# A fused SSD scan and gated feed-forward layer: the first scan in another order, and the state part of y reading the states in the scan's own tile

## The chip, the cores and the metric

The kernel runs on one core of a Trainium2 chip. The metric is the device time of one execution, in microseconds (us), over three executions: 352.07 us is their median. A core has five engines that run at the same time, each with its own list of instructions in a fixed order: TensorE (PE in the profile; its weight loads are shown apart as PEld), VectorE (DVE), ScalarE (ACT), GpSimd (POOL) and SyncE (SP), which here issues transfers. They wait for one another by semaphores.

## The reference

Two layers, one after the other, all in fp32. The first is a state-space scan (Mamba-2's SSD) for 4 sequences, 8 heads, 768 tokens, head size D = 32 and state size N = 16. The reference steps over chunks of 32 tokens:

```python
cum = np.cumsum(log_a, axis=-1)
L = np.exp(cum[:, :, :, None] - cum[:, :, None, :]) * causal
M = np.einsum('bhin,bhjn->bhij', Cc, Bc) * L
y_intra = np.einsum('bhij,bhjd->bhid', M, xc)
y_inter = np.einsum('bhin,bhnd->bhid', Cc, state) * np.exp(cum)[..., None]
y[:, :, sl] = y_intra + y_inter
decay_from_j = np.exp(cum[:, :, -1:] - cum)
Bx = np.einsum('bhjn,bhjd->bhjnd', Bc, xc) * decay_from_j[..., None, None]
state = np.exp(la.sum(-1))[:, :, None, None] * state + Bx.sum(axis=2)
```

The heads are then laid side by side, so that y is a matrix of 3072 tokens by 256, and the second layer is applied: `h = y @ w_in` (256 x 2048), `g = h * sigmoid(1.702 h)`, `out = g @ w_out` (2048 x 256).

## The kernel before

**Units of work.** The tokens are cut into six groups of 512 (`TG`). The scan works on pairs of 128-token chunks: pair p is 256 tokens, and a group has two pairs (`PG`). The chunks of the recurrence are 64 tokens (`H`), not 32, so a group has eight states. The 128 partitions hold the eight heads as four strips of 32 partitions (`r`, L-names `rows`), two heads (`q`) to a strip, 16 state elements each. A TensorE operation on one strip uses a tile of 32 rows, and four strips run side by side.

**What a group costs.** A group's y goes through `hidden` (L889: 16 slices of the 2048 hidden columns, SiLU on ScalarE) and a projection. Group 0 and part of the rest do this directly. The later groups use a product scheme with fewer multiplications (L945, L955, L1050, L1057), which needs more additions on VectorE and ScalarE. Nearly all of the time goes there.

**The weights** arrive as pairs of 32-bit words (float64) and are turned into fp32 on the chip, piece by piece: `fetch` has SyncE issue the transfers of a piece, `fields` (L192 and the line after it) cuts out exponent and mantissa on VectorE, `clamp` (ScalarE, two activations) moves the exponent, `rounded` (L208, VectorE) adds the low word, `join` (VectorE) puts it together in `w_in`. Piece 0 holds the first two hidden slices, piece 1 the third and fourth.

**Group 0's scan** is what happens before the first hidden matmul. The decays `a` are loaded, a logarithm and a cumulative sum give `cum`. Then, by engine:
- TensorE builds `cum_i - cum_j` plus a mask in PSUM for the two pairs (`mask_banks` L548, `differ` L554). Ahead of the last of them stand nine tiny matmuls, `pads` (L432), that compute nothing that is used.
- ScalarE takes the exponential (`decay_exp`, L575), which gives `L`.
- VectorE transposes C and B of the group (`turn_first`, L615). `mask_first` makes `CT`, a copy of C for each of the strip's two heads in which the other head's 16 rows are zero; `part` is the column of ones and zeros for it. GpSimd does it for both pairs (L650); for pair 1 VectorE writes one column first (L649).
- TensorE transposes B back (`turn_back`, L627), VectorE multiplies it by the decay to the end of its chunk (`ends_first`, L468, tile `Be`).
- `score` (L682, tile `cb`): C times B for every token pair of a chunk; between the two pairs' matmuls stands `since_first` (L512 on TensorE, L517 the exponential on ScalarE): the decay since the start of each chunk, tile `since`.
- `weigh` (L693, VectorE): `L` times `cb`, one instruction for each pair.
- `gain` (L713, TensorE, two PSUM banks `A`): what each chunk adds to its state, `Be` times x. Both heads of a strip are multiplied with both heads' x, so two of the four quarters of each 32 x 64 block are not wanted.
- `parts_first` (L730, ScalarE): copies `A` into `steps`, a tile [128, 64, 8] in which the eight chunks of one element lie next to each other.
- `drops` (L522, ScalarE): writes into `drop` the decay that belongs to each element of `steps`, with a zero (L724) at the first chunk of each.
- `keep_first`: one VectorE scan (L735) over `steps` and `drop` turns the eight increments into the eight states. Then ScalarE (L743, head 0) and VectorE (L744, head 1) copy the states of each pair into tiles `S`, [128, 4, 64], where the 64 elements of one state lie together, and multiply by `part`, which zeroes the unwanted quarters.
- `since_start` (L667, GpSimd, tile `CsT`): C times `since`.
- `finish`: `intra` (L833), `L` times x, into four PSUM tiles `y0_0` to `y0_3`; two of them reuse the banks that `gain` wrote and `parts_first` reads. Then `inter` (L821): the state as weights (`lhsT`, 32 rows by 64 columns), `CsT` as the moving operand, added to the same tiles. ScalarE copies the result to `yT`, and `hidden` can start. In group 1's `hidden` the 512 columns of the first two `k` steps are cut into four matmuls each, those of the next three into two.

**What sets the order.** Each engine runs its instructions in the order in which the program text issues them; the semaphores between engines follow from the tiles. The order at the end of the function (from L1166) is thus the order on each engine. The transfers for pieces 1 to 5 are issued by SyncE (`fetch(1, held=True)` and the loop after it). A one-element VectorE memset at the head of `fetch(1)` (L171) stands behind `weigh(0)`, and SyncE's transfers of that piece wait for it.

Of the kernel before, what the change touches and what calls it, by code (L numbers as in the profile page):

```python
# [16 lines left out]
P = 128  # L17
# [18 lines left out]
def kernel(  # L36
# [31 lines left out]
    nc = tc.nc  # L68
# [4 lines left out]
    NB, NH, S, D = x.shape  # L73
# [6 lines left out]
    NK = DM // P  # L80
# [4 lines left out]
    PG = CG // 2  # L85
    R = 4
    Q = NH // R
# [10 lines left out]
    ssd = ctx.enter_context(tc.tile_pool(name="ssd", bufs=2))  # L98
# [89 lines left out]
    def fields(i):  # L188
        hi, cols = bits[i][1], slice(0, PIECES[i][2] * DM)
        mantissa[i] = wide.tile([P, PN], U32, tag="m", name=f"m{i}")[:, cols]  # L190
        power[i] = wide.tile([P, PN], U32, tag="p2", name=f"p2{i}")[:, cols]
        nc.vector.tensor_scalar(out=power[i], in0=hi, scalar1=0x7FF00000, scalar2=None,  # L192
                                op0=ALU.bitwise_and)

        nc.vector.tensor_scalar(out=mantissa[i], in0=hi, scalar1=0x000FFFFF,
                                scalar2=0x00100000, op0=ALU.bitwise_and, op1=ALU.bitwise_or)

    def clamp(i):


        e = power[i]
        z = e.bitcast(FP32)
        nc.scalar.activation(z, e, AF.Relu, scale=-8.0, bias=edge[:, 0:1])
        nc.scalar.activation(e, z, AF.Relu, scale=-1.0, bias=edge[:, 1:2])

    def rounded(i):

        nc.vector.scalar_tensor_tensor(out=mantissa[i].bitcast(FP32), in0=bits[i][0],  # L208
                                       scalar=2.0 ** -32, in1=mantissa[i],
                                       op0=ALU.mult, op1=ALU.add)  # L210
# [65 lines left out]
    for r in range(R):  # L276
        (nc.sync, nc.scalar)[r % 2].dma_start(
            out=az0[32 * r:32 * r + 32].rearrange("p k s -> p (k s)"),
# [54 lines left out]
    def fold_ident(k, engine=nc.vector):  # L333
# [12 lines left out]
        out=cum.rearrange("p k s -> p (k s)"), data0=carry.rearrange("p k s -> p (k s)"),  # L346
# [13 lines left out]
    def pick_a(p):  # L360
# [34 lines left out]
    state = {}  # L395
# [69 lines left out]
    def ends_first(p):  # L465

        t = ssd.tile([P, R, 2 * Q, N], FP32, tag="Be", name=f"Be{p}", bufs=3)
        nc.vector.tensor_tensor(  # L468
            out=t, in0=rb[p],
            in1=flat[p].rearrange("p r (e i) -> p r e i", i=H)[:, :, :, H - 1:H].to_broadcast(  # L470
                [P, R, 2 * Q, N]), op=ALU.mult)
        BE[p] = t.rearrange("p r (k q) n -> p k r (q n)", k=2), t
# [46 lines left out]

    def drops():  # L520

        nc.scalar.copy(  # L522
            drop[:, :, 1:], since[0][:, :CG].rearrange("p c (s i) -> p (c s) i", s=2)[:, 1:, H - 1].unsqueeze(
                1).to_broadcast([P, Q * D, 2 * CG - 1]))

# [44 lines left out]
    def decay_exp(p, r, t):  # L570
        if p not in flat:
            L = ssd.tile([P, R, 2 * Q * H], FP32, tag="L", name=f"L{p}", bufs=3)
            flat[p] = L
            Ls[p] = L.rearrange("p r (k q i) -> p k r q i", k=2, q=Q)
        nc.scalar.activation(flat[p] if r is None else flat[p][:, r], t, AF.Exp)  # L575
# [46 lines left out]
    def turn_back():  # L622

        o = bank("b").rearrange("p (j r k e) -> p j r k e", j=PG, r=R, k=2)
        for p in range(PG):
            for k in range(2):
                nc.tensor.transpose(out=o[:, p, :, k], in_=st[p]["BT"][:, k], identity=ident)  # L627
            rb[p] = o[:, p].rearrange("p r k (q n) -> p r (k q) n", q=Q)
# [15 lines left out]
    def mask_first(p):  # L644

        s = st[p]
        s["CT"] = ssd.tile([P, 2, Q, P], FP32, tag="CT", name=f"CT{p}")
        if p:
            nc.vector.memset(s["CT"][:, 0, 0, :1], 0.0)  # L649
        nc.gpsimd.tensor_tensor(  # L650
            out=s["CT"], in0=s["tp"].unsqueeze(2).to_broadcast([P, 2, Q, P]),
            in1=part.unsqueeze(1).unsqueeze(3).to_broadcast([P, 2, Q, P]), op=ALU.mult)
# [8 lines left out]
    def since_start(p, engine=nc.vector):  # L661

        b, c = divmod(2 * p, NC)
        s = st[p]
        tp = s["tp"]
        s["CsT"] = ssd.tile([P, 2, P], FP32, tag="CsT", name=f"CsT{p}", bufs=3)
        engine.tensor_tensor(out=s["CsT"], in0=tp, in1=since[b][:, c:c + 2], op=ALU.mult)  # L667

    def score(pairs, between=lambda: None):

        cb = area(f"cb{pairs[0]}").rearrange("p r (k e) -> p r k e", k=2 * PG)
        for n, p in enumerate(pairs):
            s = st[p]
            BT, CT = s["BT"], s.pop("CT")
            s["cb"] = cb[:, :, 2 * n:2 * n + 2]
            if n:
                between()
            for k in range(2):
                for i, side in enumerate(SIDES):
                    for r in range(R):  # L680
                        rows = slice(32 * r, 32 * r + 32)
                        nc.tensor.matmul(  # L682
                            out=s["cb"][side, r, k].rearrange("p (q i) -> p q i", q=Q),
                            lhsT=BT[rows, k, side], rhs=CT[rows, k, :, side],
                            start=True, stop=True, tile_position=(32 * r, H * i),
                            skip_group_check=True)
# [38 lines left out]

    def parts_first():

        to = steps.rearrange("p e (c s) -> p s c e", s=2)
        for i in range(2):
            nc.scalar.activation(to[:, i], increment[0][i], AF.Copy)  # L730

    def keep_first():

        flat_steps = steps.rearrange("p e m -> p (e m)")
        nc.vector.tensor_tensor_scan(  # L735
            out=flat_steps, data0=drop.rearrange("p e m -> p (e m)"), data1=flat_steps,
            initial=0.0, op0=ALU.mult, op1=ALU.add)
        o = steps.rearrange("p (q d) m -> p q m d", q=Q)
        for p in range(PG):
            state[p] = ssd.tile([P, 4, Q * D], FP32, tag="S", name=f"S{p}", bufs=3)  # L740
            to = state[p].rearrange("p m (q d) -> p q m d", q=Q)
            m = slice(4 * p, 4 * p + 4)
            nc.scalar.activation(to[:, 0], o[:, 0, m], AF.Copy, scale=part[:, 0:1])  # L743
            nc.vector.tensor_scalar(out=to[:, 1], in0=o[:, 1, m], scalar1=part[:, 1:2], scalar2=None,  # L744
                                    op0=ALU.mult)

    def keep_both(pairs, by_scalar=False):

# [129 lines left out]
    def hidden(g, f):  # L878
        j, i = divmod(f, 2)
        if i == 0:  # L880
            block(g, j)
        h = bank(f"h{g}_{f}")
        for k in range(NK):
            n = 2 if g == 1 and NK * f + k < 5 else 1
            if n == 2 and NK * f + k < 2:
                n = 4
            for e in range(n):
                cols = slice(e * TG // n, (e + 1) * TG // n)
                nc.tensor.matmul(out=h[:, cols], lhsT=w_in[:, f, k], rhs=yT[g][:, k, cols],  # L889
                                 start=(k == 0 and e == 0), stop=(k == NK - 1),  # L890
                                 skip_group_check=True)

        nc.scalar.activation(gT[g, j][:, i], h, AF.Silu, scale=GELU_SCALE)
# [263 lines left out]
    def dense(n):  # L1157
        if n:
            t = bank("dense")
        for i in range(n):  # L1160
            nc.tensor.matmul(out=t[:, :4 * H], lhsT=ones,
                             rhs=ones[:, :H].unsqueeze(1).to_broadcast([P, 4, H]),
                             start=True, stop=True, skip_group_check=True)
# [4 lines left out]
        mask_banks(0, r, both[:, r])  # L1168
    for r in range(R):
        if r == R - 1:  # L1170
            pads(9, busy)
        mask_banks(1, r, bank(f"ab1_{r}"))
    turn_first("C")
    turn_first("B")
# [3 lines left out]
    mask_first(0)  # L1178
    for r in range(R):
        decay_exp(1, r, ab[1, r])  # L1180
    fields(0)
    mask_first(1)
    turn_back()
    ends_first(0)
    ends_first(1)
    score(range(PG), since_first)
    weigh(0)
    fetch(1, held=True)
    for i in range(2, 6):
        fetch(i)  # L1190
    rows_a(az, (nc.sync,))
    weigh(1)
    rounded(0)
    drops()
    gain(range(PG))
    parts_first()
    for p in range(PG):
        since_start(p, nc.gpsimd)
    clamp(0)
    keep_first()  # L1200
    dense(2)
    finish(range(PG))
    dense(0)
# [241 lines left out]
```

## Time and profile before

| what | value |
|---|---|
| three executions | 350.84, 352.07, 352.60 us; median 352.07 us |
| the profiled execution, its own time | 349.68 us |
| its span, from the first instruction to the last | 347.8 us |
| PE busy | 342.0 us, 98% of the span |
| weight loads (PEld) busy, beside PE | 271.9 us, 78% |
| DVE busy | 253.5 us, 73% |
| ACT busy | 153.1 us, 44% |
| POOL busy | 12.9 us, 4% |
| granted TensorE clock, mean | 1.000 |

The profile is of one execution. "Busy" is the time in which an engine had an instruction under way; matmuls are pipelined, so a busy TensorE isn't one at its peak. The chain of waits follows the last instruction of the program back: at each step to what released it, or to the instruction before it on its engine; "issue" is time in which an engine waited for nothing that the profile shows, and a name like DVEq is an engine's sequencer. In a line of a group, `out<-in` names the tiles, then come the sizes (partitions x elements), and a bracket gives the idle time before the group and what ended it. L numbers are lines of the kernel before.

### The profile page before, as it was taken

How to read it: one execution, taken by the hardware profiler on the slowest of the kernel's cores; microseconds unless marked ns; L12 is line 12 of the kernel's file. 1: busy time of each engine (PE TensorE's matmuls, PEld its weight loads, DVE VectorE, ACT ScalarE, POOL GpSimd, SP SyncE). 2: the span in 40 equal slices, each digit the busy share in tenths (PEclk: the TensorE clock that was granted, in tenths of full speed). 3: DMA queues.
4: the chain of work that ended last, by engine and by line, in shares of the span. 5: the costliest groups of instructions: out<-in, count | busy, mean ns of one | idle time of the engine just before them, and what ended most of it. 6: DMA issues, size and time to landing. Idle time of an engine off the chain costs nothing.

```text
span 347.8 us, 8141 instructions
## 1 busy us (share of the span) xinstructions
PE 342.0 (98%) x3392; PEld 271.9 (78%) x3392; DVE 253.5 (73%) x479; ACT 153.1 (44%) x349; POOL 12.9 (4%) x41
## 2 busy tenths in 40 slices
PE   8899999999999999999999999999999999999996
PEld 6644444557788888888888888888888888899996
DVE  5899999998679998839995649787555654455463
ACT  5698573107354324744332543442444321554320
POOL 8300000000000100000000000000000000000000
PEclk9999999999999999999999999999999999999999
DMA  6699997435526100435613036300000300000301
GB/s 162 142 336 193 283 212 155 81 77 93 105 58 128 33 2 15 63 104 102 101 28 50 2 81 117 64 2 1 2 2 2 61 2 0 0 2 0 62 0 61
DMA packets 89980, 25.92 MB, mean 75 GB/s; under 512 B 73432, under 2 KB 87128, under 8 KB 89944
## 3 DMA queue, kind: packets, MB, share of 16 engines
q1 hardware_dynamic: 89112, 24.88, 33.3%
q10 hardware_dynamic: 832, 0.52, 0.5%
q8 instruction: 26, 0.43, 0.5%
q14 instruction: 10, 0.08, 0.1%
HBM read 22.15 MB, written 3.24 MB: 73 GB/s over the span
## 4 chain that ended last, share of the span: by engine, by line
PE 97%; ACT 1%; DVE 1%; issue 0%; DVEq 0%
PE acc L1050 28%; PE X L945 20%; PE Y L955 14%; PE h L889 10%; PE o L987 8%; PE acc L1057 7%; PE y L833 2%; PE y L821 2%; PE cb L682 2%; PE A L713 1%; PE busy L440 1%; PE ab L554 1%; PE ab L548 0%; DVE steps L735 0%; ACT steps L730 0%; ACT drop L522 0%
## 5 line engine op out<-in xcount | busy, mean ns | idle before, releaser
L950 ACT ACTIVATE ac<-X 128x256 f32<-128x256 f32 x76 | 29.1, 383 | 78.6 <-PE X L945 78.2
L1050 PE MATMUL acc<-mg,mw 128*128 128x256 f32 x192 | 54.5, 379 | 0.0
L922 ACT ACTIVATE gT<-gT 128x512 f32<-128x512 f32 (+1 forms) x76 | 39.3, 520 | 34.1 <-DVE gT L1077 33.4
L1077 DVE TENSOR_TENSOR gT<-Y,ac 128x512 f32<-128x512 f32 x38 | 26.2, 689 | 36.1 <-PE Y L955 30.5
L945 PE MATMUL X<-my,mi 128*128 128x256 f32 x152 | 45.2, 380 | 0.0
L1077 DVE TENSOR_TENSOR gT<-Y,b 128x256 f32<-128x256 f32 x38 | 15.8, 419 | 35.2 <-PE Y L955 35.2
L1050 PEld LDWEIGHTS acc<-mg,mw 128*128 128x128 f32 x192 | 36.5, 190 | 5.0
L1050 PE MATMUL acc<-gT,w_out 128*128 128x256 f32 x128 | 35.5, 379 | 0.0
L889 PE MATMUL h<-yT,w_in 128*128 128x512 f32 (+2 forms) x98 | 35.5, 518 | 0.0
L945 PEld LDWEIGHTS X<-my,mi 128*128 128x128 f32 x152 | 28.0, 190 | 4.1 <-ACT ac L950 0.4
L889 PEld LDWEIGHTS h<-yT,w_in 128*128 128x128 f32 x98 | 17.0, 190 | 16.5 <-issue 14.3
L987 PE MATMUL o<-gT,w_out 128*128 128x512 f32 x64 | 28.6, 597 | 0.0
L913 DVE TENSOR_TENSOR mg<-gT 128x512 f32<-128x512 f32 x40 | 27.2, 681 | 0.0
L1050 PEld LDWEIGHTS acc<-gT,w_out 128*128 128x128 f32 x128 | 24.2, 190 | 3.4 <-ACT yT L860 0.2
L950 ACT ACTIVATE b<-X 128x256 f32<-128x256 f32 x38 | 14.6, 384 | 20.0 <-PE X L945 19.6
L945 PE MATMUL X<-yT,w_in 128*128 128x256 f32 x76 | 23.2, 389 | 0.0
L945 PE MATMUL X<-my,w_in 128*128 128x256 f32 x76 | 22.7, 382 | 0.2 <-issue 0.2
L955 PE MATMUL Y<-yT,w_in 128*128 128x256 f32 x76 | 22.7, 381 | 0.0
L955 PE MATMUL Y<-my,mi 128*128 128x256 f32 x76 | 22.6, 379 | 0.0
L955 PE MATMUL Y<-yT,mi 128*128 128x256 f32 x76 | 22.5, 379 | 0.0
L987 PEld LDWEIGHTS o<-gT,w_out 128*128 128x128 f32 x64 | 11.8, 190 | 13.2 <-issue 12.7
L402 DVE TENSOR_TENSOR_SCAN L<-a,idents 128x1024 f32<-128x1024 f32 x9 | 20.5, 2277 | 0.4 <-DMA a<-scratch 0.4
(156 smaller groups left out, 544.2 us busy)
## 6 DMA issues: line engine op xcount, KB each, us to landing
a<-scratch SPq DMA_DIRECT2D x18, 256.0 KB, 5.3
bits<-in_moe_w_out_dram SPq DMA_DIRECT2D x8, 512.0 KB, 5.4
x<-in_x_dram SPq DMA_DIRECT2D x24, 128.0 KB, 3.0
out_dram<-ob SPq DMA_DIRECT2D x40, 64.0 KB, 1.9
bits<-in_moe_w_in_dram SPq DMA_DIRECT2D x8, 256.0 KB, 4.6
bits<-in_moe_w_in_dram SPq DMA_DIRECT2D x4, 512.0 KB, 9.3
b<-in_B_dram SPq DMA_DIRECT2D x20, 64.0 KB, 3.0
af<-in_a_dram SPq DMA_DIRECT2D x3, 384.0 KB
```

The lines of the kernel that those rows point to most:

```text
L402: nc.vector.tensor_tensor_scan(out=L, data0=ra[p].rearrange("p k e -> p (k e)"), data1=idents.rearrange("p h i -> p (h i)"), initial=0.0, ...
L682: nc.tensor.matmul(out=s["cb"][side, r, k].rearrange("p (q i) -> p q i", q=Q), lhsT=BT[rows, k, side], rhs=CT[rows, k, :, side], start=Tru ...
L889: nc.tensor.matmul(out=h[:, cols], lhsT=w_in[:, f, k], rhs=yT[g][:, k, cols], start=(k == 0 and e == 0), stop=(k == NK - 1), skip_group_ch ...
L913: nc.vector.tensor_tensor(out=t[:, 0:2], in0=B[:, :, 1], in1=B[:, 0], op=ALU.subtract)
L922: nc.scalar.activation(o, i, AF.Silu, scale=GELU_SCALE)
L945: nc.tensor.matmul(out=s["X"], lhsT=lhsT, rhs=rhs, start=i == "1", stop=i == "4", skip_group_check=True)
L950: nc.scalar.activation(copy, s["X"], AF.Copy)
L955: nc.tensor.matmul(out=o, lhsT=lhsT, rhs=rhs, start=s.pop("new", False), stop=i != "5", skip_group_check=True)
L987: nc.tensor.matmul(out=o[c], lhsT=w_out[:, c, f], rhs=gT[g, f // 2][:, f % 2], start=(f == 0), stop=(f == NF - 1), skip_group_check=True)
L1050: nc.tensor.matmul(out=acc[g][0][i][:, cols], lhsT=w, rhs=h[:, cols], start=(j == 0 and k == 0 and (i, 0) in begins), stop=(j == NF // 2 - ...
L1057: nc.tensor.matmul(out=o[k] if type(o) is list else o[:, cols], lhsT=h[:, cols], rhs=w, start=(j == 0 and (i, k) in begins), stop=(j == NF ...
L1077: nc.vector.tensor_tensor(out=o, in0=v, in1=w, op=ALU.add)
```

## The change

Ten edits, nearly all in group 0's scan:
1. `drops` runs on GpSimd instead of ScalarE.
2. `CT` of pair 1 is made by VectorE in two instructions (one for each head, C times a column of `part`), not by GpSimd; the one-column memset goes.
3. `parts_first` is four ScalarE activations instead of two, one for each half chunk and head, and each multiplies by `part`. So the unwanted quarters are zero before the scan.
4. The copies L743 and L744 behind the scan go. `state[p]` is a view into `steps`: the weights of `inter` are read there, with a step of eight fp32 elements (32 bytes) from one column to the next. Pair 2, in the next group, reads the last of these states in the same way.
5. `since_first`, `drops` and both `since_start` move up to right after `turn_back`, ahead of `ends_first` and `score`; `since_first` no longer stands between the two pairs' `cb` matmuls.
6. `mask_first(1)` stands ahead of `fields(0)`.
7. `clamp(0)` stands ahead of `weigh(0)`, and so, on ScalarE, ahead of `parts_first`.
8. `rounded(0)` stands behind the scan instead of ahead of `gain`.
9. `pads` is 15 tiny matmuls instead of 9.
10. In group 1's `hidden`, the first three `k` steps are cut into two matmuls each, none into four, and the fourth and fifth not at all.

```diff
     def drops():
-        nc.scalar.copy(
+        nc.gpsimd.tensor_copy(
             drop[:, :, 1:], since[0][:, :CG].rearrange("p c (s i) -> p (c s) i", s=2)[:, 1:, H - 1].unsqueeze(
                 1).to_broadcast([P, Q * D, 2 * CG - 1]))
...
         if p:
-            nc.vector.memset(s["CT"][:, 0, 0, :1], 0.0)
+            for q in range(Q):
+                nc.vector.tensor_scalar(out=s["CT"][:, :, q], in0=s["tp"], scalar1=part[:, q:q + 1],
+                                        scalar2=None, op0=ALU.mult)
+            return
         nc.gpsimd.tensor_tensor(
...
     def parts_first():
-        to = steps.rearrange("p e (c s) -> p s c e", s=2)
+        to = steps.rearrange("p (q d) (c s) -> p s q c d", s=2, q=Q)
         for i in range(2):
-            nc.scalar.activation(to[:, i], increment[0][i], AF.Copy)
+            o = increment[0][i].rearrange("p c (q d) -> p q c d", q=Q)
+            for q in range(Q):
+                nc.scalar.activation(to[:, i, q], o[:, q], AF.Copy, scale=part[:, q:q + 1])
...
         for p in range(PG):
-            state[p] = ssd.tile([P, 4, Q * D], FP32, tag="S", name=f"S{p}", bufs=3)
-            to = state[p].rearrange("p m (q d) -> p q m d", q=Q)
-            m = slice(4 * p, 4 * p + 4)
-            nc.scalar.activation(to[:, 0], o[:, 0, m], AF.Copy, scale=part[:, 0:1])
-            nc.vector.tensor_scalar(out=to[:, 1], in0=o[:, 1, m], scalar1=part[:, 1:2], scalar2=None,
-                                    op0=ALU.mult)
+            state[p] = steps.rearrange("p e m -> p m e")[:, 4 * p:4 * p + 4]
...
-            n = 2 if g == 1 and NK * f + k < 5 else 1
-            if n == 2 and NK * f + k < 2:
-                n = 4
+            n = 2 if g == 1 and NK * f + k < 3 else 1
...
-            pads(9, busy)
+            pads(15, busy)
...
+    mask_first(1)
     fields(0)
-    mask_first(1)
     turn_back()
+    since_first()
+    drops()
+    for p in range(PG):
+        since_start(p, nc.gpsimd)
     ends_first(0)
     ends_first(1)
-    score(range(PG), since_first)
+    score(range(PG))
+    clamp(0)
     weigh(0)
...
     weigh(1)
-    rounded(0)
-    drops()
     gain(range(PG))
     parts_first()
-    for p in range(PG):
-        since_start(p, nc.gpsimd)
-    clamp(0)
     keep_first()
+    rounded(0)
```

More of the change, by code (lines that the diff above doesn't have):

```diff
@@ L737, in keep_first @@
             initial=0.0, op0=ALU.mult, op1=ALU.add)
-        o = steps.rearrange("p (q d) m -> p q m d", q=Q)
         for p in range(PG):
-            state[p] = ssd.tile([P, 4, Q * D], FP32, tag="S", name=f"S{p}", bufs=3)
-            to = state[p].rearrange("p m (q d) -> p q m d", q=Q)
-            m = slice(4 * p, 4 * p + 4)
-            nc.scalar.activation(to[:, 0], o[:, 0, m], AF.Copy, scale=part[:, 0:1])
-            nc.vector.tensor_scalar(out=to[:, 1], in0=o[:, 1, m], scalar1=part[:, 1:2], scalar2=None,
-                                    op0=ALU.mult)
+            state[p] = steps.rearrange("p e m -> p m e")[:, 4 * p:4 * p + 4]
     def keep_both(pairs, by_scalar=False):
```

## The prediction

> **What bounds the kernel now.** I read the chain of work that ended last first, by engine, because it says whether the end is set by one engine:
>
> ```profile
> PE 97%; ACT 1%; DVE 1%; issue 0%; DVEq 0%
> ```
>
> The rest is in the first 18 us. From the first hidden-layer matmul (L889, at 17.79) TensorE is busy without a gap worth naming: 42.00 of the 42 us from 18 to 60, 40.00 of 40 from 60 to 100, 244.81 of 248 after that (busy time by stretch). The granted clock is 1.00 in every stretch. So the change is worth what it moves the start of L889, as long as the weights that L889 reads keep up. Second view: the same chain in order of time, from 9 to 18 us.
>
> ```profile
> 10.00 0.68 PE rows L512 x4
> 10.68 0.65 ACT since L517 x2
> ...
> 11.35 1.01 ACT drop L522
> 12.36 1.02 ACT steps L730 x2
> ...
> 13.64 0.69 DVE m L208
> 14.32 1.15 DVE steps L735
> ...
> 15.49 0.59 DVE S L744 x2
> ...
> 16.12 1.68 PE y L821 x54
> 17.79 0.68 PE h L889
> ```
>
> The columns are start and duration. Three things stand there that the change takes out: `drop` on ScalarE, `m` (L208) ahead of the scan (L735), and the state copies (L744, L743 beside it) between scan and state part (L821). Third view: the timeline of the engines around it.
>
> ```profile
> 11.36 2.36 DVE L693 TENSOR_TENSOR L<-L,cb 128x1024 f32<-128x1024 f32 x2 [1.12 <-PE cb L682]
> 12.27 1.11 ACT L730 ACTIVATE steps<-A 128x256 f32<-128x256 f32 x2
> 15.49 0.94 ACT L743 ACTIVATE S<-steps,part 128x128 f32<-128x128 f32 x2 [0.90 <-DVE steps L735]
> 15.49 0.58 DVE L744 TENSOR_SCALAR S<-steps,part 128x128 f32<-128x128 f32 x2
> 17.69 0.43 DVE L192 TENSOR_SCALAR p<-bits 128x512 uint32<-128x512 uint32 x1
> ```
>
> The reader should see that VectorE is nearly as late as ScalarE: `weigh` (L693) ends at 13.72, L730 at 13.38. Taking `drop` away alone gains nothing.
>
> **The change part by part.** Each term against this execution: span 347.8, its own time 349.68.
>
> *Six more pads* (9 to 15). The 18 records of the nine pads take 0.37 with 0.21 for one, so about 9 ns each; 12 more records put the next group (L554) 0.1 later, and with it the exponentials and `turn_back`. The clock is granted in full already, so I count no gain.
>
> *Rows first, C's second mask by VectorE.* Transposes start 0.1 later, at 8.82; the next group follows 0.59 later as now (8.72 to 9.31). `rows` goes there: 9.41 instead of 9.93. `since` follows 0.73 after `rows` (9.93 to 10.66), so 10.14 to 10.80, about 0.5 earlier. The two `cb` groups come after it at about 10.04, without the 0.33 wait for GpSimd's mask and with fewer changes of tile shape (each shows 0.17 to 0.2 of "issue"): the second ends about 11.16 instead of 11.25. `weigh(0)` waits for the last matmul of the second group in both kernels, so it starts 0.09 earlier, at 11.27. VectorE pays two 128x256 masks, 0.295 each by the nearest row (L341), between `turn_first` and `fields`; the covers are its own wait of 1.12 for `cb`, and for the first hidden weights the stretch up to 15. Without that cover it would cost 0.5.
>
> *`drop` to GpSimd.* 448 elements with a strided source are in no GpSimd row. Bounds: 0.56 at the rate of a memset (L540, 256 in 0.32), 1.3 at that of L667 (256 in 0.74). It waits for `since` and ends by 12.2 at the latest, and the two L667 behind it by 13.7; the scan wants `drop` at 13.8 and L821 wants L667's result at 15.5. Cost nothing; the cover is 1.6 us.
>
> *`clamp(0)` ahead of `parts_first`.* 1.43 of ScalarE (13.16 to 14.59), now from about 10.7 to 12.1. It fills the wait for `gain`, which does not move: its last matmuls began at 11.81, just after the last `x` transfer signalled at 11.77. So `parts_first` starts at 12.27, as now.
>
> *`parts_first` in four.* The same 512 elements in the same strided pattern, with a scale. Lower bound 1.11 (the two now), upper 4 x 0.66 = 2.64 if nothing overlaps. Starts lie 0.20 apart for L767 (64 elements, eight in 1.70) and 0.42 for L743 (128 elements, strided on one side). I take 0.34, nearer to L743: 12.27 + 3 x 0.34 + 0.52 = 13.81, which is **0.43 later** than now.
>
> *The scan without L208 before it.* It needs `weigh(1)` (13.55) and `parts_first` (13.84 with the wait): 13.84 instead of 14.24, ends 15.06 instead of 15.46. L208 comes after it, 0.60, and `join(0)` starts at 15.66 instead of 15.99.
>
> *The state copies go.* 0.59 of VectorE and 0.94 of ScalarE. What is late next is not the scan but the intra-chunk part on TensorE (L833): two of its four PSUM tiles take over the banks that `parts_first` reads, one half each, and the last of these is free only when `parts_first` ends. Now its second wave starts at 13.42 and ends at 15.42, with a pause of 0.63 in it (14.05 to 14.69) that the trace puts to "issue". From 13.86 it ends at 15.22 without that pause, 15.85 with it; I take 15.5. So L821 starts at **15.5 instead of 16.12: 0.62 gained**.
>
> *L821 reads the states where the scan left them*, one element in eight, 32 bytes apart. No matmul or weight load in this trace reads like that, so its price is bounded. Now a weight load pays 0.89 ns a column (190 ns for 128 columns at L889, 133 for 64 here), and L821 goes in 28 rounds of 52 ns, which is one load of 64 columns: 1.46 us from first start to last. Below, a strided load is free: 1.46. Above, the rows are the two engines that read this very tile with this step. VectorE: L744 takes 331 ns for 128 elements, a 12-element copy (L357) 170, so 1.39 ns an element. ScalarE: L743's starts are 0.42 apart for 128 elements, as far as L659's are for 256 contiguous ones (four in 1.70), so twice the price an element, about 1.9 ns; with nothing set aside as fixed it is 3.3 ns. I take VectorE's 1.39, as it lies between free and ScalarE's: 64 x 1.39 = 89 ns a round, 2.49 us, **1.03 lost**.
>
> [...]
>
> *Sum.* 15.5 + 2.49 + 0.2 to the next tile shape = 18.19 for L889 instead of 17.78: +0.41. A wait of 0.03 at the third hidden slice (weights ready at 21.19, matmul at 21.34) goes: -0.03. The split in `hidden(1)`: 16 records 0.112 apart become 8 that are 0.2155 apart: -0.07. Pair 2 reads the last state with stride in four matmuls, two rounds: +0.06. Together **+0.37**: 350.05 for this execution. The profiled execution is 2.39 below the median of the three runs, 352.07; the same shift on that gives 352.4.
>
> **The rivals.**
>
> *A. Strided loads are free.* L889 could start at 15.5 + 1.46 + 0.2 = 17.16. But the third slice's weights then bound: VectorE's L192 at 17.69 followed a transfer that signalled at 17.59, and that transfer is issued after `weigh(0)`, which moves only 0.09. So the 0.62 on TensorE shrinks to 0.12, with the split -0.2: 351.9. [...] Against: L743 and L744.
>
> *B. ScalarE's 1.9 ns holds.* 122 ns a round, 3.4 us; L889 at 19.1, +1.3 in all: 353.4.
>
> *C. Slower by more than 0.5%.* The weight loads pay L743's whole 3.3 ns a column: 210 ns a round, 5.9 us; L889 at 21.6: +4.0 with pair 2's rounds, 356.1. This decides once a round passes 135 ns, that is 2.1 ns a column. For it: nothing overlaps a load here, since each round is exactly one load. Against: VectorE reads the same tile at 1.39.
>
> *D. The four `parts_first` do not overlap.* They end at 14.91; L833 at about 16.6, L889 at 19.3: +1.5, 353.6.
>
> *E. The change does not shorten the chain:* scan and intra part wait for `parts_first`, so taking out `drop` and L208 yields nothing. That is within the forecast already (0.40 at the scan, 0.62 at L821).
>
> **How the numbers follow.** Forecast 36%, A 33%, B 12%, C 13%, D 6%. The forecast's own range is 351.7 to 353.0. The range takes in A to D without C and the spread of the runs shown (350.84 to 352.6): 350.8 to 354.5, with C's 13% and a few per cent below left out. 0.5%, 1.76 us, is about what a measurement of this kernel can tell from no change. No case is faster by that much; I leave 7% for something not seen. Slower by it: C, and the top of B and D, 18%. Within it: 75%.
>
> **What would show it.** In the profile after: `since` near 10.1; `parts_first` ending near 13.8; scan at 13.8, right behind `weigh`; L821 starting near 15.5, and its records 89 ns a round (52 if A, 122 if B, over 135 if C); L889 at 18.2. I would be wrong if L833 is late for another reason than `parts_first`, if VectorE's masks delay Be beyond 11.1, or if TensorE gets gaps after 18 us that it does not have now.

## The result and the profile after

The changed kernel takes 352.86 us (median of 22 executions, 351.12 to 355.24); the kernel before, run beside it, 351.26 us (median of 22, 349.70 to 353.27). The ratio is **1.0049, with a 95% interval of 1.0035 to 1.0063**: about 1.7 us slower. The forecast was +0.37 us, with a range (350.8 to 354.5) that holds the measured time. That its 352.4 us lies so near to 352.86 is luck: it was counted from the median of three executions, 352.07, and the median of 22 is 351.26.

The profile after is of the longest of those 22 executions (355.24 us, span 353.4). One thing in it has to be set aside first. TensorE got its full clock at 10.34 us (4.37 in the profile before); this is where the trace's record of a full clock begins, and for the time ahead of it, which has no record, the profile prints 1.00. Ahead of 10.34 the same matmuls are slower: L554 takes 4.22 us instead of 2.59, and everything behind it stands 2.6 us later. L548's matmuls start 0.213 us apart there, and 0.109 apart behind the 4.37 us of the profile before. In the nine other profiles with fifteen pads in which the full clock is recorded it came between 4.15 and 6.57, so the late clock seems to belong to that execution rather than to the change. So I compare from the first matmul of `turn_back` (L627) on, which both kernels reach with all earlier work done. The chain of waits of the changed kernel, start and duration:

```profile
11.29 0.65 PE b L627 x4
11.94 0.65 PE rows L512 x4
12.60 1.14 PE cb L685 x63
13.73 0.79 PE A L716 x53
14.52 1.06 PE dense L1158 x4
15.58 1.02 PE y L832 x63
16.60 0.14 issue
16.73 0.84 PE y L832 x52
17.58 3.08 PE y L820 x56
20.66 6.59 PE h L886 x11
```

ScalarE and VectorE are gone from this chain: neither `drop`, nor `m`, nor the scan, nor copies of the states stand in it. From turn_back to the first hidden matmul it is TensorE alone, and the largest piece is the state part, L820, at 3.08 us (1.68 before). The first hidden matmul comes 9.30 us after turn_back; before it was 9.06. Shares by engine of the whole chain say the same:

```profile
PE 98%; issue 0%; DVE 0%; ACT 0%
```

The second thing to see is the granted clock in the stretches around the state part (columns: stretch, length, busy time of TensorE with its matmuls, clock, DMA share, GB/s):

```profile
17.17:20.58 3.41, 3.41 (x90) 1.00 0.99 258
20.58:23.99 3.41, 3.41 (x6) 0.50 0.95 290
24.00:27.00 3.00, 3.00 (x8) 1.00 1.09 385
```

Right behind the state part the clock is halved for 3.41 us: six hidden matmuls where at full clock there are eight in 3.0. That is not chance in this one execution. The mean clock of an execution tells whether it had such a stretch (3.41 us at half speed in 350 gives 0.995): **16 of the 22 executions of the changed kernel had it, and 15 of the 81 of the kernel before whose clock is listed.** The 16 take 353.38 us on average, the other six 351.94. In the kernel before, the 15 are 0.46 us longer on average than the other 66; no profile shows where in them the clock was low.

### The profile page after: what moved, and what is told of

Read it like the earlier page. It is cut to its first block, busy times and chain, and to the rows that moved or that the text cites. A ratio compares the mean times of both kernels' runs of the same rounds, so it can differ in the third digit from the quotient of the medians.

```text
span 353.4 us, 8142 instructions
## 1 busy us (share of the span) xinstructions
PE 347.3 (98%) x3392; PEld 275.0 (78%) x3392; DVE 253.4 (72%) x478; ACT 151.7 (43%) x348; POOL 12.9 (4%) x41
## 4 chain that ended last, share of the span: by engine, by line
PE 98%; issue 0%; DVE 0%; ACT 0%
PE acc L1047 27%; PE X L942 19%; PE Y L952 14%; PE h L886 10%; PE o L984 8%; PE acc L1054 7%; PE y L832 3%; PE y L820 2%; PE cb L685 2%; PE A L716 1%; PE ab L554 1%; PE busy L440 1%; PE ab L548 1%; PE dense L1158 0%; PE tp L597 0%
## 5 line engine op out<-in xcount | busy, mean ns | idle before, releaser
L1074 DVE TENSOR_TENSOR gT<-Y,b 128x256 f32<-128x256 f32 x38 | 15.8, 418 | 35.9 <-PE Y L952 35.9
L886 PE MATMUL h<-yT,w_in 128*128 128x512 f32 (+1 forms) x86 | 37.0, 587 | 0.0
```

The costliest lines, as they stand in the source:

```text
L1074: nc.vector.tensor_tensor(out=o, in0=v, in1=w, op=ALU.add)
```

## The experiments

Theory (load and clock): a weight load that reads one element in eight is slow (L820 goes in rounds of 120 ns, L821 before in rounds of 52), and the long, thin stretch that this makes leads to the halved clock. Rival one (start): the loss is at the start of the kernel, in the pads and the order. Rival two (order): the halved clock comes from the new order, not from the reads. Each ratio is to the kernel before, run beside the kernels of the same batch (e1 to e4, e5 to e8, e9 to e12), each batch on a chip of its own.

The table gives, from the one profile of each kernel, when the full clock came, when turn_back and the first hidden matmul began, the time between these two, and the state part from its first matmul's start to its last's; then the executions with a mean clock below 0.9975 and the ratio to before.

| kernel | full clock | turn_back | hidden | between | state part | clock lowered | ratio (95%) |
|---|---|---|---|---|---|---|---|
| before | 4.37 | 8.72 | 17.78 | 9.06 | 1.46 | 15 of 81 | 1 |
| changed | 10.34 | 11.29 | 20.59 | 9.30 | 2.88 | 16 of 22 | 1.0049 (1.0035-1.0063) |
| e1 | 4.49 | 9.10 | 17.96 | 8.86 | 1.46 | 0 of 12 | 1.0018 (0.9996-1.0040) |
| e2 | 4.49 | 9.16 | 19.16 | 10.00 | 2.87 | 7 of 12 | 1.0026 (1.0007-1.0045) |
| e3 | 6.04 | 9.55 | 18.20 | 8.65 | 1.63 | 0 of 12 | 0.9995 (0.9976-1.0015) |
| e4 | 6.25 | 9.56 | 18.07 | 8.51 | 1.46 | 0 of 12 | 1.0015 (0.9996-1.0033) |
| e5 | 6.12 | 9.56 | 19.29 | 9.73 | 2.87 | 1 of 1 | one execution |
| e6 | 4.83 | 9.05 | 17.39 | 8.34 | 1.50 | 0 of 1 | one execution |
| e7 | 4.85 | 9.06 | 19.80 | 10.74 | 4.31 | 5 of 7 | 1.0190 (1.0165-1.0214) |
| e8 | not recorded | 9.52 | 18.19 | 8.67 | 1.63 | 0 of 12 | 0.9992 (0.9974-1.0010) |
| e9 | 4.15 | 8.71 | 17.27 | 8.56 | 1.46 | 1 of 12 | 1.0008 (0.9979-1.0037) |
| e10 | 6.01 | 9.42 | 17.73 | 8.31 | 1.46 | 0 of 12 | 0.9956 (0.9933-0.9979) |
| e11 | 6.57 | 9.66 | 24.28 | 14.61 | 7.73 | 6 of 6 | 1.0302 (1.0260-1.0345) |
| e12 | 5.16 | 9.21 | 17.73 | 8.52 | 0.83 | 2 of 12 | 1.0050 (1.0022-1.0078) |

### e1: the copies put back

```diff
-            state[p] = steps.rearrange("p e m -> p m e")[:, 4 * p:4 * p + 4]
+            state[p] = ssd.tile([P, 4, Q * D], FP32, tag="S", name=f"S{p}", bufs=3)
...
+            nc.scalar.activation(to[:, 0], o[:, 0, m], AF.Copy, scale=part[:, 0:1])
+            nc.vector.tensor_scalar(out=to[:, 1], in0=o[:, 1, m], scalar1=part[:, 1:2], scalar2=None,
+                                    op0=ALU.mult)
```

> The changed kernel, with the two copies behind the scan put back, so that the states are read without gaps again; all other edits stay. [...] Then the rounds of L821 are 52 ns again, the first hidden matmul comes about 8.7 us after turn_back (9.4 changed, 9.1 before), the mean clock is 1.000 in nearly all executions, and the ratio to before is 0.997 to 1.001. Rival one (start): the loss is at the start, where TensorE is at half speed until 10.3 us in the profile after, and the later dip is chance: ratio 1.004 as in the changed kernel, whatever L821 does. Rival two (order): the dip comes from the new order, not from the reads: clock 0.995 in most executions still, ratio 1.003 to 1.005.

Measured: 351.79 us (median of 12), ratio 1.0018. The clock is 1.000 or 0.999 in all 12, the state part is back at 1.46 us. So in the changed kernel the halved clock is due to the reads, as the theory has it, and rival two falls. But the ratio is above what the theory gave: with the reads mended, about 0.6 us of loss may be left (the interval reaches from none to 1.4). Its chain shows where a part goes:

```profile
15.18 5.42 DMA bits<-in_moe_w_in_dram
...
20.69 0.43 DVE p L192
21.12 0.34 DVE m L195
21.46 0.61 DVE p L222
...
22.09 0.70 DVE w_in L228
...
22.93 2.38 PE h L892 x5
```

The third hidden slice (L892 at 22.93) could have begun at 21.5 and waits for its weights. L192 here is `fields` of piece 2, which waits for the transfer of piece 2 (20.60), and `join` of piece 1, the one that the third slice needs, stands behind it on VectorE. The execution without the slow reads is held by the next thing in line. This would also explain why the six executions of the changed kernel at full clock (351.94 on average) are no slower than e1 (351.96): the slow loads' time there would lie beside this wait. That is argued, as no profile shows one of the six.

### e2: the reads alone

The kernel before, with `parts_first` in four as in the change, and:

```diff
-            nc.scalar.activation(to[:, 0], o[:, 0, m], AF.Copy, scale=part[:, 0:1])
-            nc.vector.tensor_scalar(out=to[:, 1], in0=o[:, 1, m], scalar1=part[:, 1:2], scalar2=None,
-                                    op0=ALU.mult)
+            state[p] = steps.rearrange("p e m -> p m e")[:, 4 * p:4 * p + 4]
```

> The kernel before, with only parts_first in four and the states read in the scan's tile (edits 3 and 4). Load and clock: L821 starts about 0.4 earlier than before, goes at 120 ns a round for about 2.9 us, the first hidden matmul is 0.5 to 0.9 later than before, the clock is 0.995 in over half of the executions: ratio 1.004 to 1.007. Rival one (start): the nine pads are as before, so ratio 0.999 to 1.002 and a clock of 1.000. Rival two (order): 1.001 to 1.003, clock 1.000.

Measured: 351.92 us, ratio 1.0026; clock lowered in 7 of 12 (352.59 us on average, the other five 351.48). So the reads bring the halved clock without the new order as well, though less surely than in e1: the kernel before, beside it, has a lowered clock in 8 of 35. The one profile of e2 is of an execution at full clock, so where the clock falls in the others isn't shown. The ratio is below what was expected, but its interval reaches into it.

### e3: four strips abreast

```diff
+            for n, p in enumerate(pairs):
+                inter(n, p)
             for t in range(NK):
-                for n, p in enumerate(pairs):
-                    inter(n, p, (t,))
```

> The changed kernel, but the state part is issued for both halves of y before either half is copied, so that the four strips' loads stand next to each other instead of two and two. [...] If the four loads share one path, a round takes 240 ns, nothing is gained: ratio 1.004 to 1.006, clock 0.995 in most. Rival one (start): 1.002 to 1.004.

Measured: 350.92 us, ratio 0.9995, clock 1.000 in all 12. The loads are as slow as in the changed kernel, but four run side by side. The weight loads of the state part, first of the changed kernel, then of this one (shortest, median and longest in ns, first and last start in us):

```profile
L820 PEld LDWEIGHTS y<-CsT,steps x56: 189/212/213, 17.5 to 20.3; 32*64 32x64 f32 x56
```

```profile
L820 PEld LDWEIGHTS y<-CsT,steps x56: 189/212/213, 15.8 to 17.3; 32*64 32x64 f32 x56
```

The same 212 ns a load, and half the time for all 56. So the price belongs to each strip's load, not to a path that the strips share, and slow loads alone do not lower the clock: 1.6 us of them, four strips abreast, did not; 2.9 us of them, two abreast, did. Whether the length or the width of the stretch counts, this run doesn't tell (e11 was to part them). The first hidden matmul comes 8.65 us after turn_back; from 14 rounds of about 120 ns, 1.7 us, I had expected 8.2.

### e4: seven steps instead of the scan

```diff
-        nc.vector.tensor_tensor_scan(
-            out=flat_steps, data0=drop.rearrange("p e m -> p (e m)"), data1=flat_steps,
-            initial=0.0, op0=ALU.mult, op1=ALU.add)
+        for m in range(1, 2 * CG):
+            e = m % 2 * H + H - 1
+            nc.vector.scalar_tensor_tensor(
+                out=steps[:, m], in0=steps[:, m - 1], scalar=since[0][:, m // 2, e:e + 1],
+                in1=steps[:, m], op0=ALU.mult, op1=ALU.add)
```

> The changed kernel, with the increments laid out state by state and the scan replaced by seven scalar_tensor_tensor steps of 64 elements (the form that later groups use, 284 ns each before); no drop, no copies, no gaps in what the weight loads read. Load and clock: the seven steps take 2.0 us instead of 1.2, but the first pair's states are there after three, so L821 starts behind L833 as in the changed kernel and runs at 52 ns a round as states come; first hidden matmul 8.0 to 8.4 us after turn_back, clock 1.000, ratio 0.996 to 0.999 (capped by the third hidden slice's weights). Rival one (start): 1.002 or more.

Measured: 351.61 us, ratio 1.0015. The steps take 2.21 us, the state part is fast, the clock 1.000 or 0.999 in all; but the hidden matmul comes 8.51 us after turn_back, and TensorE then stands idle for 1.77 us until the third slice's weights are there, as in e1 (1.27). The expected gain did not come; in the profile this wait takes more than all of it.

### e5 and e6: a step of 16 and of 8 bytes

Copies as in e1, into another layout: four states side by side in e5 (first line added), two in e6 (the other two; `ByTwo` picks state m as `[m // 2, m % 2]`). The figure to look at is the time of one weight load, 133 ns before and 212 in the changed kernel.

```diff
-            state[p] = ssd.tile([P, 4, Q * D], FP32, tag="S", name=f"S{p}", bufs=3)
+            state[p] = ssd.tile([P, Q * D, 4], FP32, tag="S", name=f"S{p}", bufs=3).rearrange("p e m -> p m e")
...
+            t = ssd.tile([P, 2, Q * D, 2], FP32, tag="S", name=f"S{p}", bufs=3)
+            state[p] = ByTwo(t.rearrange("p a e b -> p a b e"))
```

> The changed kernel with copies behind the scan into one tile for each pair in which the four states of a pair lie next to each other: a weight load reads every fourth element, 16 bytes apart (32 bytes in the changed kernel, 4 with plain copies). A look at the weight load's duration and at the rounds. [...] If it grows with the distance, the load lies between 133 and 212 ns, near 155.

> [...] If any gap in the read costs, about 212 ns. If it grows with the distance, near 140 ns.

Measured, in this order: the loads of before (4 bytes from column to column), of e6 (8 bytes) and of e5 (16 bytes).

```profile
L821 PEld LDWEIGHTS y<-CsT,S x56: 128/133/133, 16.1 to 17.5; 32*64 32x64 f32 x56
```

```profile
L836 PEld LDWEIGHTS y<-CsT,S x56: 130/133/133, 15.7 to 17.1; 32*64 32x64 f32 x56
```

```profile
L826 PEld LDWEIGHTS y<-CsT,S x56: 187/211/212, 16.2 to 19.0; 32*64 32x64 f32 x56
```

133, 133, 211, and 212 at 32 bytes in the changed kernel. It is a step between 8 and 16 bytes, not a slope: a price that grows with the distance was expected to give about 140 and 155. The rise is 78 to 79 ns on 64 columns; what makes it, no run shows.

The clock in e5, in the stretch of its state part and the one behind it:

```profile
16.36:19.77 3.41, 3.41 (x57) 1.00 0.99 268
19.77:23.18 3.41, 3.41 (x5) 0.50 0.95 305
```

In both profiles the halved stretch lasts 3.41 us, and it begins a whole number of 3.41 us after the full clock came: 10.34 + 3 x 3.41 = 20.58 in the changed kernel, 6.12 + 4 x 3.41 = 19.77 here. I read that as a clock that changes in steps of 3.41 us, counted from the full clock: an estimate from these two profiles. TensorE shows as busy for the whole 3.41 us ahead of each halved stretch, so what lowered the clock is no standstill that the profile counts.

Such steps would explain why not every execution is hit. In e2's profile the state part is as long and as slow, and the clock stays full. Counted from its 4.49 us, one step ends and the next begins at 18.14, within the state part (16.08 to 18.95), so that neither is filled by it. No experiment moved the state part against these steps; this rests on three profiles.

```profile
18.00:21.00 3.00, 3.00 (x27) 1.00 0.97 257
```

### e7: more for TensorE to do beside the slow loads

```diff
+                    if early:
+                        for t in ts:
+                            rows = slice(64 - 64 * t, 96 - 64 * t)
+                            nc.tensor.matmul(
+                                out=filler[:Q * D, t, :P], lhsT=zeros[rows],
+                                rhs=ones[rows], start=True,
+                                stop=True, tile_position=(64 - 64 * t, 0), skip_group_check=True)
```

> The changed kernel, with one more matmul in each round of L820, on a strip of rows that the round does not use: zeros as weights, ones as the moving operand, 128 columns, written into a bank that nobody reads (the output does not change). The slow loads stay; only TensorE has more to do beside them. [...] Rival (the clock drops for another reason than idle arrays in the state part): clock 0.995 in about 70% still, ratio 1.005 or more.

Measured: 357.30 us (7 executions), ratio 1.0190; clock lowered in 5 of 7, in four of them by twice as much (0.990). So the filler did not keep the clock up in most executions, and the theory in its simple form (more matmuls beside the slow loads, full clock, ratio 1.001 to 1.003) fails. The one profile, though, is of one of the two executions at full clock. In it the 3.41 us from 15.09 to 18.50 (counted from 4.85) hold 2.65 us of state part with filler and 0.57 us of standstill, as much together as the state part with slow loads had in the 3.41 us that half speed followed (3.1 in the changed kernel, 2.9 in e5), and the clock stays full:

```profile
15.00:18.00 3.00, 2.93 (x94) 1.00 0.97 286
18.00:21.00 3.00, 2.07 (x22) 1.00 1.00 291
```

So where it can be read, the filler did what the theory says; where the clock fell in the other five isn't shown. The run does not speak for the rival either, since it brought in something else: the state part got longer, 4.31 us, with a hole in it (start, duration; in brackets the idle time before):

```profile
17.66 0.27 PE L831 MATMUL filler<-ones,zeros 32*64 32x128 f32 x1
18.93 0.26 PE L831 MATMUL filler<-ones,zeros 32*64 32x128 f32 x1 [1.00 <-issue]
```

This hole stands behind TensorE's 961st record (matmuls, weight loads and waits, counted in order of time); in all 14 profiles but one (e2) there is a jump of 0.35 to 1.1 us from one start to the next right behind the 705th, in the middle of the intra-chunk part. The two are 256 apart. TensorE's program comes in packets of 16 KB, one for 256 records:

```profile
q8 instruction: 26, 0.43, 0.5%
```

(queue, packets, MB, share, from the page after.) In this kernel such a packet moved from 16.24 to 17.56, and TensorE went on at 18.93, 1.38 later. Before the change the packet moved from 12.16 to 13.24 and TensorE went on at 14.69, 1.44 later. All fifteen such holes are alike (the 705th record in 13 profiles, the 961st in e7 and e11): TensorE goes on 1.23 to 1.50 after the packet has moved. In e2 the packet had moved 1.36 before TensorE needed it, and there is no hole. So the pause of 0.63 us in L833, which the prediction could only call "issue", is TensorE waiting for its code.

### e8: join of piece 1 first

```diff
+    join(1)
     fields(2)
     clamp(2)
-    join(1)
```

> The kernel with four strips abreast, and join of piece 1 ahead of fields of piece 2 at the end of the scan, so that the weights of the third and fourth hidden slice no longer wait on VectorE for the transfer of piece 2. In the profile of the four abreast the third slice began at 22.32, 0.58 after the second could have ended; the wait is up to 1.4 in the other profiles. If that wait is what ate the gain on the state part: third slice at 21.7 to 21.9 by the same clock, ratio 0.997 to 0.999. If not, ratio as without it, 0.9995.

Measured: 350.65 us, ratio 0.9992 (four abreast without it: 0.9995). The third slice no longer waits (its weights are there at 21.50, and its first matmul comes at 21.73, the regular 0.43 after the one before), but the time hardly moves, at the upper end of what I expected or beyond it. The wait of 0.58 us was real in the profile of e3; whether taking it out gains anything can't be told from these two ratios, whose intervals are 0.2% to either side.

### e9 and e10: fifteen pads and nine

e9 is e1 with `join(1)` ahead of `fields(2)`, as in e8. e10 has, in addition:

```diff
-            pads(15, busy)
+            pads(9, busy)
```

> The changed kernel with the copies behind the scan put back, and join of piece 1 ahead of fields of piece 2. With the copies alone the mean clock was 1.000 in all 12 executions and the ratio still 1.0018 (0.9996 to 1.0040); its profile shows the third hidden slice 1.4 late, behind piece 2's transfer. If that wait is the rest of the loss, it goes: third slice without a wait, ratio 0.998 to 1.000. If the rest of the loss is at the start (pads, rows first), ratio 1.001 to 1.003.

> The same with nine pads instead of fifteen, as in the kernel before. By the count of records six pads cost 0.1 us. If the pads decide when TensorE gets its full clock (it was reached between 4.4 and 10.3 us in the profiles), the time moves by more than 0.5 us either way. I expect less than 0.3 us against the kernel with fifteen.

Measured: 351.08 us with fifteen pads (ratio 1.0008), **349.58 us with nine (ratio 0.9956)**, twelve executions each on the same chip. Six matmuls of 32 x 32 cost 1.5 us between the medians, fifteen times the 0.1 that the prediction gave them, and against what I expected of the run. (The two intervals only touch, at 0.9979, so that the pads cost something is clear and how much is not.) So rival one was right about the pads. In the two profiles, though, the time isn't lost at the start: they are nearly of one speed from turn_back to the hidden matmul (8.56 and 8.31). After it the kernel with fifteen pads falls back in three places: by 0.19 in the first 15 us, by 0.37 at 100 us, by 0.79 at 241 us (counted from its first hidden matmul). At 100 us TensorE waits for ScalarE (L953). In e9 the third slice still comes 0.39 late, as in e10, so join first shortened that wait and did not end it. The last of the three places, with fifteen pads and with nine:

```profile
258.63 0.43 PE Y L958 x2
259.06 0.52 issue
259.58 0.70 PE Y L958 x2
```

```profile
258.51 0.86 PE Y L958 x4
259.37 0.43 PE X L948 x2
```

The hole is behind TensorE's record 5825, that is 705 + 20 x 256: the seam between two packets of code again. Fifteen pads leave 60 records and nine 36, so other matmuls stand at every later seam. That the six pads cost time here is shown; that the seams are the reason is argued from one profile of each, and not settled: e2 has nine pads and a hole of 0.65 at the same seam, the kernel before one of 0.16, and the kernels with fifteen pads and as many records ahead of it have holes from 0.16 (e3) to 0.96 (the changed kernel). A second candidate is the start: e9 has four of twelve executions above 352.5, e10 none, and a late full clock, as in the profile after, would do that. Of the profiles only the one of the changed kernel shows such a start.

### e11: the state part twice

```diff
-                for n, p in enumerate(pairs):
-                    inter(n, p, (t,))
+                for _ in range(2):
+                    for n, p in enumerate(pairs):
+                        inter(n, p, (t,))
```

> The changed kernel with the copies put back, and the state part issued twice, so that it is counted twice in y. Its loads are fast (52 ns a round) and it lasts about as long as the slow one, 2.9 us. If the clock drops because two strips of 32 rows keep too little of the array at work, whatever the loads cost, the clock is 0.995 in over half of the executions, ratio 1.004 to 1.007. If it drops because TensorE idles between slow loads, the clock is 1.000 nearly always, ratio 1.002 to 1.004.

Measured: 361.63 us (6 executions), ratio 1.0302, the clock 0.981 to 0.991 in all. It was meant to part long and thin from slow, and cannot: the longer program puts the seam behind the 961st record inside the state part, and there TensorE stands still.

```profile
16.37 1.90 PE y L826 x63
18.27 3.26 issue
21.53 2.82 PE y L826 x25
```

The packet of code moved from 17.21 to 20.16 among the weights' transfers, 2.95 us for 16 KB, and TensorE went on 1.37 later. Here the 3.41 us ahead of the halved clock (16.8 to 20.2) hold a true standstill.

### e12: all of it together

The edits of e4, e3 and e8 together, and:

```diff
+    fetch(1, held=True)
     weigh(0)
-    fetch(1, held=True)
```

> What the runs point to, together: the seven steps instead of the scan (no gaps in the weight loads, no copies), the state part four strips abreast, join of piece 1 ahead of fields of piece 2, and the transfers of piece 1 released ahead of the first weigh instead of behind it. State part 0.8 to 1.2 us, the first hidden matmul about 8.1 us after turn_back, the weights of the third slice there in time, clock 1.000: ratio 0.997 to 0.9985. If the earlier transfers collide with the last of x, gain follows late and the ratio is 0.999 to 1.001.

Measured: 352.83 us, ratio 1.0050, executions from 350.32 to 356.99: a miss. The state part is the shortest of all (0.83 us), but the hole at the 705th record is the longest (1.11), after the weights' transfers were released earlier; but e4, without that, has 1.03. The profile is of the shortest of the twelve executions, so it does not show what the others lose. This stays open. It has fifteen pads, as e4 and e8 have.

The best kernel of the study is e10: copies kept, the new order, nine pads, join of piece 1 first. At 0.9956 (0.9933 to 0.9979) it is faster than both, by 0.4% and 0.9%.

## Why the prediction came out as it did

The forecast said slightly slower, for the reason that the gain on the chain is given back by slow weight loads. Up to the first hidden matmul the chain came out as forecast, in part by luck; the time did not stop there. Step by step, times from turn_back's first matmul:

- **Rows first, `since`**: forecast 1.32 after turn_back, measured 1.32 (12.605 - 11.285). Right. `weigh` forecast 2.45, measured 2.48. Right.
- **`drop` on GpSimd**: bounded by 0.56 and 1.3, measured 0.98, done 1.7 us before the scan. Right, it costs nothing.

```profile
13.32 0.98 POOL L522 COPY drop<-since 128x448 f32<-128x448 f32 x1 [4.46 <-ACT since L517]
14.27 1.42 POOL L670 TENSOR_TENSOR CsT<-Ct,since 128x256 f32<-128x256 f32 x2
```

- **`parts_first` in four, behind `clamp(0)`**: forecast 1.54 for the four, measured 1.28 (a start every 0.26, not 0.34).

```profile
13.91 0.72 ACT L204 ACTIVATE p<-p,edge 128x512 uint32<-128x512 f32 x1
14.54 1.28 ACT L735 ACTIVATE steps<-A,part 128x128 f32<-128x128 f32 x4
```

- **The scan without L208 ahead of it**: it ends 5.98 after turn_back, forecast 6.24; `m` (L208) comes behind it. VectorE is no longer late:

```profile
13.77 2.36 DVE L696 TENSOR_TENSOR L<-L,cb 128x1024 f32<-128x1024 f32 x2 [0.96 <-PE cb L685]
14.94 0.06 DVE L171 MEMSET bits<- 128x1 uint32 x1
16.05 1.22 DVE L740 TENSOR_TENSOR_SCAN steps<-drop,steps 128x512 f32<-128x512 f32 x1
17.19 0.67 DVE L208 SCALAR_TENSOR_TENSOR m<-bits,m 128x512 f32<-128x512 uint32 x1
```

- **L833 bounds the state part's start**: forecast 6.68 after turn_back, measured 6.22 (17.50 - 11.285). The mechanism was right, and the earlier end of `parts_first` explains most of the difference.
- **The strided loads**: the price was between free and dear as the prediction had it, but the term was undersized. Forecast 89 ns a round, from VectorE's 1.39 ns an element; measured 120 ns, as rival B had it (122). The state part took 2.88 from first to last start, forecast 2.49; B's 3.4 was too much because rounds of the two halves of y overlap for a few rounds.
- **First hidden matmul**: forecast 9.37 after turn_back, measured 9.30. That is luck: two errors of 0.4 against each other.
- **Rival A's cap** (the third slice's weights hold back any gain on the state part) was real: in e1 and e4, with fast loads, TensorE stood idle for 1.27 and 1.77 us there.

What failed is two steps that were priced by their own duration alone. *"So the change is worth what it moves the start of L889"*: that the clock is 1.00 in every stretch of the profile before was taken to hold for the changed kernel. (For the first 4.37 us it was no more than printed.) In the two profiles that show the clock fall with slow loads, the state part filled 3.1 us (changed kernel) and 2.9 us (e5) of the 3.41 ahead, and the clock was 0.50 for the next 3.41. The changed kernel's executions with that stretch are 1.44 us longer than those without, and they are 16 of 22: 1.05 us on average, as much as the difference between the changed kernel and e1 (1.07, uncertain by 0.9). And the pads' term, 0.1: they cost 1.5 us in e9 against e10. A sign that the prediction named for being wrong, gaps in TensorE's work after 18 us, is there too: from 100 us on TensorE is without work for 4.2 us in the changed kernel's profile, for 3.0 in the one before.

```profile
100.00:348.00 248.00, 244.81 (x2097) 215.07 (x2096) 165.72 (x328) 95.68 (x239) 1.38 (x5) 1.00 0.20 39
100.00:354.00 254.00, 249.22 (x2238) 218.70 (x2237) 169.98 (x338) 99.43 (x248) 1.38 (x5) 1.00 0.21 39
```

(Before, then changed: length, then busy time of PE, PEld, DVE, ACT and POOL. The last 0.2 and 0.6 us of the stretches lie behind the end.)

On the other side the rest of the change was worth more than forecast. e10 has the new order, without the strided reads and the pads, and is 1.5 us faster than before. (It has join of piece 1 first as well, worth 0.03% by e3 and e8 and 0.1% by e1 and e9, both within their intervals.) So the sum is roughly: all other edits together -1.3, pads +1.5, strided reads by way of the clock +1.05, together +1.25, against a measured +1.7 that is uncertain by 0.5. The pads' term is taken over from the kernel with copies; fewer pads with the strided reads were not tried. The split of the hidden matmuls into fewer pieces was not tried by itself.

Not settled: what in such a stretch lowers the clock (e7 and e11 changed the code's seams as well), what makes a weight load dear from 16 bytes on, why six pads cost so much, whether they cost it in the changed kernel too, and what e12 loses in most executions.

## What to carry to other kernels

Before an operand is read in place to save a copy, look at its step: TensorE's fp32 weight loads were no longer at 8 bytes than at 4 and 1.6 times as long at 16 and 32, and issuing four strips abreast instead of two hid nearly all of that again (1.63 us against 1.46). A stretch of thin work is priced by what follows it too: with 2.9 us of slow two-strip matmuls, 16 of 22 executions had 3.4 us at half clock. And instructions that compute nothing need not be cheap: six of them cost 1.5 us here, for a reason that is still open. Test a few of them more or less by themselves before they are believed to cost their own duration.

## What the runs showed of the hardware

- A weight load of 32 rows by 64 columns in fp32 takes 133 ns at a step of 4 or 8 bytes, 211 to 212 ns at 16 or 32; four strips' loads do not slow one another (56 loads from 15.8 to 17.3 us in e3, against 17.5 to 20.3).
- With a state part of 2.9 us the mean clock shows a stretch at half speed in 16 of 22 executions (changed kernel) and 7 of 12 (e2); in the two profiles that hold it (changed kernel, e5) it is 3.41 us right behind the state part. With the same loads and a state part of 1.6 us it is in none of 24 (e3, e8).
- TensorE takes its program in packets of 16 KB, one for 256 records (26 packets, 0.43 MB); a packet that came late stopped it for 0.1 to 3.3 us, and it went on 1.23 to 1.50 us after the packet had moved (fifteen holes).
